# Score products of two heads' keys per partition half, and diagonal blocks of 192 columns, in a kernel of two attention layers and two linear-attention layers

## The chip, the core and the metric

The kernel runs on one core of a Trainium2 chip. The core has a matrix engine (TensorE, PE in the profile, with its weight loads listed apart as PEld), a vector engine (VectorE, DVE), a scalar engine that evaluates functions such as exp (ScalarE, ACT), a general engine (GpSimd, POOL), a queue engine that issues transfers (SyncE, SP), and 16 DMA engines. Products land in PSUM, which the kernel uses as four buffers of 128 partitions x 1024 four-byte values. The metric is the device time of one execution in microseconds (us).

## What is computed

The reference applies four layers to 2048 tokens of width 512: an attention layer A, a linear layer B, and both once more. Each layer is `x = x + layer(layernorm(x))`. A has 32 heads of 16 and works in four segments of 512 tokens. Cut to what matters here:

```
logits = einsum('bhqd,bhkd->bhqk', qs, ks) * scale + mask      # mask: -1e9 where key > query
p      = softmax(logits)
a_dot  = einsum('bhqk,bhkd->bhqd', p, vs)
a_mem  = (phi(qs) @ M) / (phi(qs) @ z + 1e-6)                  # M, z: sums over earlier segments
o      = g * a_mem + (1 - g) * a_dot                           # then o @ wo
M, z   = M + phi(ks)^T vs, z + sum(phi(ks))
```

The mask is causal inside a segment: of the 4 x 4 blocks of 128 queries by 128 keys, six lie wholly below the diagonal, four lie on it and need the triangle, and six are left out. B exponentiates projected keys and queries with both signs and contracts them over all tokens.

## The kernel before, in words

**How it is ordered.** The program is first written as a graph of operations (`Graph.op`), each with a planned duration, the tiles that it reads and writes, and the engines that may run it. `Graph.forward` then plays the graph with these durations and fixes the order on each engine and, where an operation may run on two engines, the engine. The list `STEPS` holds seeds: each moves some priorities before the last play (`Graph.moved`). `Graph.emit` writes the result out as one fixed instruction list per engine with semaphore waits. An operation marked `port` is not started by the planner on DVE while POOL works, and POOL is not given work while DVE runs such an operation. So a changed graph, planned duration or seed list gives a new order everywhere. The planner can also put in filler products (line 955) where PE would stand idle.

**Tiles.** Heads are taken in two sets `hp` of 16 heads; a set has two groups `gg` of 8 heads, 8 x 16 = 128 partitions. Partitions 0 to 63 hold four heads (half `b` = 0), 64 to 127 the other four. Nearly every product uses 64 partitions only, and two products, one per half, are issued together (a pair) and run at the same time in the two halves of the array.

**Scores, in `a_att` (line 1041).** For query block `i` (128 queries), group `gg` and key block `j <= i`, one pair of products writes the tile `S` in PSUM: 128 keys on the partitions, 2 halves x 4 heads x 128 queries = 1024 columns. The weights are 128 columns of `KT` (all four heads' keys of the half); the streamed side is `Q4`, in which each of the four heads has its own 512-column copy of the queries with the other three heads' partitions zero (lines 1000 to 1012: by a DMA into zeroed tiles for all segments but the first, by a DVE product with a mask `M4` for the first). ACT then writes `exp(0.25 S)` into a tile `PT` (line 1066, recorded at line 633). For `j == i`, POOL zeroes what lies above the diagonal with two `affine_select` operations of 128x512 (line 1070). There are 320 such tiles in the program, 2 layers x 4 segments x 4 groups x (1+2+3+4), and 128 of them are diagonal.

**Values.** Once all `PT` tiles of a set `hp` are there, the `PV` products (line 1092, 34 columns each, weights from `PT`, values `VT` streamed) run in two phases, in which the two partition halves of the keys swap places; the result is normalised by DVE (lines 1095 to 1099), transposed by a DMA (line 646), multiplied with `wo` and added to `X`.

**Buffers.** Of 27 tiles of 128x1024 in pool `p2`, at most 14 may be `PT`; `S` has at most 2 of the four PSUM buffers.

**Other work on the engines.** ACT also evacuates some projections, does the exps of B and copies (line 641, 633); POOL also does two small operations per layer norm (lines 886 and 888); SP issues all transposes and copies in one order.

## Time and profile before

| | |
|---|---|
| median of 4 runs | 534.22 us (530.71 to 537.62) |
| the profiled execution | 536.28 us, of which the profile's span is 534.4 us |
| granted TensorE clock, mean | 0.992 of full speed |
| instructions | 24584 |

The profile comes from one execution. "Busy" of PE counts a product from its start to its modelled end, and products overlap, so a busy PE may still have room. The chain of waits follows the work that ended last back to the start. A group of instructions carries the line that recorded it, and nearly all products are recorded at line 623, so groups are told apart by the tiles: `pQ,pK` are the scores, `pV,p` the value products.

### The profile page before, as it was taken

What the parts mean: (1) busy time and instruction counts of PE and PEld (TensorE: products, weight loads), DVE (VectorE), ACT (ScalarE), POOL (GpSimd) and SP (SyncE); (2) the same over time, 40 slices, a digit from 0 to 9 for tenths busy, and PEclk for the clock granted to TensorE, in tenths of its full rate; (3) what the DMA queues carried; (4) which work ended last, traced back from release to release, by engine and by line L of the source; (5) the groups of instructions that cost most, each with busy time, mean ns of one, the idle gap of its engine ahead of it and who ended that gap; (6) DMA issues with size and microseconds to landing.
All of it is one profiled execution on the core that took longest, in us unless ns stands there. A gap on an engine that the chain in (4) does not pass through costs nothing.

```text
span 534.4 us, 24584 instructions
## 1 busy us (share of the span) xinstructions
PE 474.2 (89%) x11148; PEld 279.5 (52%) x11148; DVE 437.9 (82%) x856; ACT 464.3 (87%) x543; POOL 231.7 (43%) x401
## 2 busy tenths in 40 slices
PE   6888977889989898999898997989989989999986
PEld 2435443454555464556656554555555546565674
DVE  5699994998977776786898998899888788887872
ACT  2699986799999999866988999999999999957993
POOL 5494994043753654200207734663564474320000
PEclk9999998999999999999999999999999999999999
DMA  4306743533111012000024434422311111100254
GB/s 125 114 13 137 163 124 86 91 43 82 42 43 42 15 36 39 12 2 2 5 61 98 93 78 74 63 57 57 72 33 29 49 22 23 33 12 3 53 120 130
DMA packets 89624, 31.77 MB, mean 59 GB/s; under 512 B 76688, under 2 KB 89520, under 8 KB 89520
## 3 DMA queue, kind: packets, MB, share of 16 engines
q1 hardware_dynamic: 89456, 30.17, 26.6%
q8 instruction: 88, 1.44, 1.2%
q14 instruction: 16, 0.13, 0.1%
q0 software_dynamic: 64, 0.02, 0.0%
HBM read 6.32 MB, written 2.10 MB: 16 GB/s over the span
## 4 chain that ended last, share of the span: by engine, by line
PE 44%; ACT 21%; DVE 19%; DMA 9%; SPq 3%; issue 2%; POOL 2%; ACTq 0%; POOLq 0%
PE D L623 42%; ACT p L633 18%; DMA p<-p 6%; DMA pX<-p 2%; DVE p L1098 2%; DVE stats L878 2%; SPq L646 1%; DVE pV L642 1%; DVE p L642 1%; DVE X L1131 1%; DVE p L899 1%; DVE pS L1176 1%; POOL p L1070 1%; DVE p L1271 1%; DVE pS L679 1%
## 5 line engine op out<-in xcount | busy, mean ns | idle before, releaser
L633 ACT ACTIVATE p<-D 128x1024 bf16<-128x1024 f32 (+1 forms) x420 | 401.1, 1030 | 38.9 <-PE D L623 35.4
L1070 POOL TENSOR_SCALAR_AFFINE_SELECT p<-p 128x512 bf16<-128x512 bf16 x256 | 162.4, 661 | 140.9 <-ACT p L633 140.2
L623 PE MATMUL D<-pQ,pK 64*128 64x512 bf16 x678 | 124.2, 378 | 8.7 <-ACT p L633 6.4
L623 PE MATMUL D<-pV,p 64*128 64x34 bf16 (+1 forms) x5316 | 93.6, 177 | 5.6 <-DVE X L1131 1.8
L623 PEld LDWEIGHTS D<-pV,p 64*128 64x128 bf16 x5316 | 81.9, 93 | 21.1 <-POOL p L1070 5.0
L886 POOL TENSOR_SCALAR rstd<-mv 128x1 f32<-128x1 f32 x60 | 17.9, 300 | 95.1 <-DVE mv L879 92.4
L623 PEld LDWEIGHTS D<-pQ,pK 64*128 64x128 bf16 x678 | 32.8, 93 | 40.6 <-ACT p L633 20.5
L1098 DVE TENSOR_TENSOR p<-D,pS 128x256 bf16<-128x256 f32 x112 | 46.7, 420 | 2.5
L623 PE MATMUL D<-WA_o,p 64*128 64x256 bf16 x512 | 39.4, 270 | 8.6 <-DMA p<-p 4.4
L1176 DVE TENSOR_REDUCE pS<-p 128x64 f32<-128x1024 bf16 (+1 forms) x36 | 38.8, 1090 | 8.4 <-ACT p L633 8.3
L878 DVE BATCH_NORM_STATS2 stats<-X 128x6 f32<-128x512 bf16 x64 | 43.3, 682 | 1.8 <-ACT X L641 1.1
L623 PE MATMUL D<-WB_o,p 64*128 64x256 bf16 x512 | 37.9, 270 | 5.4 <-DMA p<-p 4.3
L1196 DVE TENSOR_TENSOR pT<-D,pT 128x1024 bf16<-128x1024 f32 x32 | 38.7, 1216 | 3.6 <-PE D L623 3.3
L623 PE MATMUL D<-WB_k,pX 64*128 64x512 bf16 (+1 forms) x288 | 33.8, 353 | 5.7 <-DMA pX<-p 3.2
L888 POOL TENSOR_TENSOR rstd<-rstd,mhalf 128x1 f32<-128x1 f32 x60 | 34.5, 581 | 3.7
L623 PE MATMUL D<-WA_v,pX 64*128 64x512 bf16 x256 | 33.1, 377 | 2.7 <-DVE p L1098 1.0
L623 PE MATMUL D<-WB_v,pX 64*128 64x512 bf16 (+1 forms) x290 | 33.6, 353 | 1.1 <-DVE X L1131 0.4
L623 PEld LDWEIGHTS D<-WA_o,p 64*128 64x128 bf16 x512 | 21.7, 94 | 23.5 <-DMA p<-p 9.2
L623 PE MATMUL D<-pX,WB_q 64*128 64x512 bf16 x256 | 32.6, 377 | 0.3
L1131 DVE TENSOR_TENSOR X<-X,D 128x512 bf16<-128x512 bf16 x32 | 21.9, 683 | 13.2 <-PE D L623 13.0
L642 DVE CAST p<-D 128x1024 bf16<-128x1024 f32 (+2 forms) x27 | 26.2, 970 | 7.4 <-PE D L623 7.2
L679 DVE RECIPROCAL pS<-D 128x32 f32<-128x32 f32 (+1 forms) x64 | 20.7, 325 | 13.9 <-PE D L623 13.5
(115 smaller groups left out, 692.1 us busy)
## 6 DMA issues: line engine op xcount, KB each, us to landing
pQ<-p SPq DMA_DIRECT2D x56, 64.0 KB, 1.9
out_dram<-X SPq DMA_DIRECT2D x16, 128.0 KB, 2.0
X<-in_A_x_dram SPq DMA_DIRECT2D x3, 512.0 KB, 6.1
pX<-in_B_wqkv_dram SPq DMA_DIRECT2D x3, 512.0 KB, 4.5
p<-p SPq DMA_TRANSPOSE x76, 2.5
pX<-p SPq DMA_TRANSPOSE x54, 2.4
X<-in_A_x_dram SPq DMA_DIRECT2D x4, 128.0 KB, 2.9
pX<-in_A_wk_dram SPq DMA_DIRECT2D x2, 256.0 KB, 4.3
```

The costliest lines, as they stand in the source:

```text
L623: ins = e.matmul(out_ap, lhsT, rhs, start=st, stop=sp, tile_position=(basep(lhsT), 0))
L633: return self.g.op({"act": (dur, lambda e: e.activation(out_ap(), in_ap(), func, scale=scale))}, reads, writes, opens, label=label)
L642: "dve": ((340 if fast else n / 0.96 + 65), lambda e: e.tensor_copy(out_ap(), in_ap()))}
L679: return e.reciprocal(o, i)
L878: v(lambda e: e.bn_stats(self.stats[:, t, :], self.X[:, t, :]), 602, [R("X", t)], [R("st", t)], label="bn")
L886: v(lambda e: e.tensor_scalar(rs, self.mv[:, t, 1:2], LN_EPS, None, op0=ALU.add), 170, [R("mv", t)], [R("rstd", t)], eng="pool", label="rstd")
L888: v(lambda e: e.tensor_tensor(rs, rs, self.mhalf[:], ALU.pow), 540, [R("rstd", t), R("mhalf")], [R("rstd", t)], eng="pool", label="rstd")
L1070: v(lambda e, pt4=pt4: e.affine_select(pt4(), pt4(), [[0, 4], [1, 128]], ALU.is_ge, 0.0, base=0, channel_multiplier=-1), 560, [PT], [PT[hh ...
L1098: v(lambda e, pvv=pvv, rden=rden, part=part, dst=dst, k=k: e.tensor_tensor(part(dst), pvv()[:, :, k, :, 0:16], rden()[:, :, k, :, None].to ...
L1131: self.v(lambda e: e.tensor_tensor(xt(), xt(), res(), ALU.add), 602, [R("X", t), ps], [R("X", t)], label="res")
L1176: fn = lambda e, sgn=sgn, ev=ev, Z=Z, nz=nz: e.tensor_reduce(Z.t[:, sgn * nz:(sgn + 1) * nz], ev().rearrange("p (h d) -> p h d", d=16), AX ...
L1196: v(lambda e, Vt=Vt, src=src, vt=vt: e.tensor_tensor(vt(Vt, 0, 16), src(), vt(Vt, 16, 17).to_broadcast([128, 2, 2, 2, 16, 8]), ALU.mult), ...
```

## The change

Three things are redone around the scores, and buffers, planned durations and seeds go with them.

*Keys instead of queries are masked.* `KT` becomes a passing tile. The four heads of a half are split into two pairs. A new tile `KD` (128x2048) holds, for every 128 keys, twice 128 columns: the early 64 keys once for each head pair, then the late 64 keys once for each, with the other pair's partitions zero. Two `tensor_scalar` operations write it (POOL or DVE). The queries `Q2` (128 x 2 x 2 x 512) have two copies instead of four. One product then gives 64 keys for two pairs of heads at once, so a block below the diagonal takes two pairs of products of 256 columns instead of one of 512. In the result the partition half says both which 64 keys and which head pair a row is.

*Diagonal blocks are narrower.* The early 64 keys meet 128 queries, the late 64 keys only the later 64, so a half has 2 x 192 columns, `exp` covers 768 columns instead of 1024, and the columns that are never written stay zero in four tiles `PD` of their own, zeroed once. The triangle is added before the exp by a third pair of products: `II` (two stacked identities) times `far` (0 or -32768).

*Values for swapped halves.* Half of the heads now need their values in the other partition half. A DMA copies them from `VT` to a new tile `VU`, in pieces of 34 values (68 bytes).

```diff
+    def scores(self, S, PT, KD, Q2, gg, j, i):
+        c, n = gg * 1024 + j * 256, i * 128
+        def phases():
+            def item(b, m):
+                half = lambda x: x[64 * b:64 * b + 64]
+                q, k = half(Q2.t)[:, gg], half(KD.t)
+                if j < i:
+                    return S.t[:, 512 * b + 256 * m:512 * b + 256 * m + 256], k[:, c + 128 * m:c + 128 * m + 128], q[:, :, n:n + 128], m == 0, m == 1
+                out = S.t[:, 512 * b:512 * b + 384].rearrange("p (k c) -> p k c", k=2)
+                if m == 0:
+                    return out[:, :, 64:192], k[:, c:c + 128], q[:, :, n:n + 128], True, False
+                if m == 1:
+                    return out[:, :, 0:64], k[:, c + 128:c + 256], q[:, :, n + 64:n + 128], False, False
+                return out[:, :, 0:128], half(self.II), half(self.far)[:, None, :].to_broadcast([64, 2, 128]), False, True
+            return [[tuple(item(b, m) for b in range(2)) for m in range(2 if j < i else 3)]]
...
+            self.act(lambda: PT.t[:].rearrange("p (b k c) -> p b k c", b=2, k=2)[:, :, :, 64:256],
+                     lambda: S.t[:].rearrange("p (b c) -> p b c", b=2)[:, :, 0:384].rearrange("p b (k c) -> p b k c", k=2),
+                     ACT.Exp, 768, [S], [PT], scale=0.25, label="exp")
...
-                    PT = PTs[(gg, j)] = self.T(self.p2, "PT")
-                    self.mm(lambda S=S, KT=KT, Q4=Q4, j=j, gg=gg: [[tuple(
-                        (S.t[:, b * 512:(b + 1) * 512], KT.t[64 * b:64 * b + 64, gg * 512 + j * 128:gg * 512 + (j + 1) * 128],
-                         Q4.t[64 * b:64 * b + 64, gg, :, i * 128:(i + 1) * 128], True, True) for b in range(2))]],
-                        [[512]], [KT, Q4[("i", gg, i)] if (L, s) in MASKED else (Q4, ALLKEYS)], [S], opens=[PT], label="S")
-                    self.act(lambda PT=PT: PT.t[:], lambda S=S: S.t[:], ACT.Exp, 1024, [S], [PT], scale=0.25, label="exp")
-                    if j == i:
-                        for hh in range(2):
-                            pt4 = lambda PT=PT, hh=hh: PT.t[:, hh * 512:(hh + 1) * 512].rearrange("p (h q) -> p h q", h=4)
-                            v(lambda e, pt4=pt4: e.affine_select(pt4(), pt4(), [[0, 4], [1, 128]], ALU.is_ge, 0.0, base=0, channel_multiplier=-1),
-                              560, [PT], [PT[hh]], eng="pool", label="mask")
+                    PT = PTs[(gg, j)] = self.T(self.p2, "PT") if j < i else self.T(self.pP, "PD")
+                    self.scores(S, PT, st["KD"][hp], st["Q2"][hp], gg, j, i)
...
+            for m in range(2):
+                def fn(e, KT=KT, KD=KD, m=m, raw=raw):
+                    dst = KD.t[:].rearrange("p (t x c) -> p t x c", x=4, c=64)
+                    dst = dst[:, :, 0::3] if m else dst[:, :, 1:3]
+                    return e.tensor_scalar(dst, KT.t[:].rearrange("p (t x c) -> p t x c", x=2, c=64), self.MK[:, 0 if raw else 1, m:m + 1], None, op0=ALU.mult)
+                self.g.op({"pool": (1250.0, fn), "dve": (600.0, fn)}, [KT, R("MK0") if raw else R("MK1")], [KD[m]], label="KD", port=True)
...
-                for b in range(2):
-                    for i in range(4):
-                        fn = lambda e, Q4=Q4, QT=QT, i=i, b=b: e.tensor_tensor(
...
-                for a in range(0, 4, 2):
-                    fn = lambda e, Q4=Q4, QT=QT, a=a: [e.dma_start(Q4.t[sl::4, :, sl, :], QT.t[sl::4, :].rearrange("p (b q) -> p b q", b=2)) for sl in (a, a + 1)]
+                    fn = lambda e, Q2=Q2, QT=QT, k=k: e.tensor_scalar(Q2.t[:, :, k, :], QT.t[:].rearrange("p (b q) -> p b q", b=2), self.MQ[:, k:k + 1], None, op0=ALU.mult)
...
+                fn = lambda e, Q2=Q2, QT=QT: [e.dma_start(Q2.t[k::2, :, k, :], QT.t[k::2, :].rearrange("p (b q) -> p b q", b=2)) for k in range(2)]
...
+            self.dma(lambda tp=tp: [(VU.t[64 - 64 * h:128 - 64 * h, 2 * tp:2 * tp + 2].rearrange("p t (u r) c -> p t u (r c)", r=2),
+                                     VT.t[64 * h:64 * h + 64, 2 * tp:2 * tp + 2].rearrange("p t (u k r) c -> p t u k (r c)", k=2, r=2)[:, :, :, 0])
+                                    for h in range(2)], 2, [VT[2 * tp], VT[2 * tp + 1]], [VU[2 * tp], VU[2 * tp + 1]], label="Vx", lat=4000.0)
...
-N_XT, N_Q4, N_K1, N_K2, N_VT, N_SM, N_KT = 5, 3, 12, 27, 5, 6, 4
+N_XT, N_Q4, N_K1, N_K2, N_VT, N_SM, N_KT, N_PD = 5, 3, 12, 23, 5, 6, 4, 4
-CAP2 = {"PT": 14, "EQ": 16, "ET": 8, "phe": 2, "phiKT": 2, "QT": 2, "PhK": 2, "phiQ": 4}
+CAP2 = {"PT": 7, "EQ": 16, "ET": 8, "phe": 2, "phiKT": 2, "QT": 2, "KT": 2, "PhK": 2, "phiQ": 4}
```

Not printed: the setup of `II`, `far`, `MQ`, `MK` and of the zeros in `PD`; the index arithmetic of `PV`, which reads the new places; planned durations of loads (520 to 560, 620 to 640) and of the two POOL operations of a layer norm (170 to 240, 540 to 560); and `STEPS`, whose 148 seeds are replaced by 212 others. The instruction lists of the two kernels count:

| engine | before | after | what differs most |
|---|---|---|---|
| PE | 11150 | 12006 | scores 678 to 1312, triangle 256, fillers and warm-up 170 to 132 |
| ACT | 545 | 550 | 128 of the 320 attention exps are 128 x 4 x 192; more copies of weights, fewer of `X` |
| DVE | 858 | 848 | 16 masked query products go, 4 `KD` and 4 `Q2` come |
| POOL | 405 | 186 | 256 selects go, 28 `KD` come |
| SP | 239 | 243 | query copies 56 to 28, value copies 32 |

## The prediction, made before the changed kernel had run

> **What bounds the kernel now.** The first view is the page's busy times, with the chain that ended last.
>
> ```profile
> PE 474.2 (89%) x11148; PEld 279.5 (52%) x11148; DVE 437.9 (82%) x856; ACT 464.3 (87%) x543; POOL 231.7 (43%) x401
> PE 44%; ACT 21%; DVE 19%; DMA 9%; SPq 3%; issue 2%; POOL 2%; ACTq 0%; POOLq 0%
> L1070 POOL TENSOR_SCALAR_AFFINE_SELECT p<-p 128x512 bf16<-128x512 bf16 x256 | 162.4, 661 | 140.9 <-ACT p L633 140.2
> ```
>
> Three engines are above 80%, so the average names no bound. The second view, busy time by stage, does (columns: stretch, its length, busy us and calls of each engine, clock, DMA share, GB/s).
>
> ```profile
> 27.00:75.00 48.00, 42.24 (x990) 22.70 (x988) 45.67 (x99) 47.04 (x54) 39.57 (x66) 1.00 0.48 104
> 75.00:95.00 20.00, 13.16 (x184) 5.85 (x178) 11.87 (x21) 13.96 (x15) 10.90 (x18) 0.91 0.47 108
> 107.00:160.00 53.00, 48.33 (x1238) 28.19 (x1232) 47.48 (x88) 51.63 (x56) 27.28 (x46) 1.00 0.28 52
> 160.00:214.00 54.00, 47.44 (x1276) 28.03 (x1272) 39.87 (x75) 51.16 (x55) 27.05 (x48) 1.00 0.16 33
> 267.00:320.00 53.00, 49.06 (x1055) 30.07 (x1049) 48.81 (x107) 47.80 (x59) 24.50 (x46) 1.00 0.37 82
> 320.00:374.00 54.00, 48.23 (x1138) 27.44 (x1136) 48.64 (x98) 51.28 (x55) 29.37 (x50) 1.00 0.35 64
> 374.00:427.00 53.00, 48.64 (x1270) 28.84 (x1266) 44.95 (x79) 51.49 (x55) 27.70 (x48) 1.00 0.23 46
> 427.00:455.00 28.00, 25.41 (x744) 15.35 (x744) 22.82 (x44) 27.84 (x31) 17.00 (x31) 1.00 0.14 22
> 455.00:481.00 26.00, 25.47 (x584) 15.35 (x582) 22.49 (x38) 20.12 (x23) 6.75 (x13) 1.00 0.10 23
> ```
>
> The numbers are PE, PEld, DVE, ACT, POOL. In the six stretches 107-214 and 267-455, 295 us together, ACT works 281.2 us, 95%: it is the bound there, with 13.8 us idle. In 27-75 ACT (98%) and DVE (95%) are. In 75-95 no engine is: in the chain of waits SP's queue (75.0 to 81.0) and a transpose (3.64 us from 81.08) stand there. In 455-481 PE is. How full PE really is needs the third view, products back to back in the timeline (start, duration).
>
> ```profile
> 377.60 0.96 PE L623 MATMUL D<-pV,p 64*128 64x34 bf16 x64
> 380.76 1.04 PE L623 MATMUL D<-pX,WA_q 64*128 64x512 bf16 x8
> 393.57 0.61 PE L623 MATMUL D<-WA_o,p 64*128 64x256 bf16 x8
> ```
>
> Eight products are four pairs: 0.43 us more for 4 x 256 more columns is 0.42 ns a column, and 0.61 us less 4 x 107 ns leaves 0.18 us, one tail, with nothing per pair. Thirty-two pairs of 34 columns take 0.96 us, 25 ns a pair after the tail. Counting every form of each stretch by these two rules, max(0.42 ns x columns, 25 ns) a pair, PE needs 44.7, 43.4, 46.2, 44.7, 45.4 and 22.2 us in the six ACT-bound stretches: 246.6 of 295, 84% (1.4 of it fillers), and 24.2 of 26, 93%, in 455-481, the fullest stretch seen.
>
> **The change part by part**, against the profiled execution: 536.28 us, span 534.4, so 1.9 lies around the span, and it is 2.06 above the median of the runs.
>
> *Narrower exps.* The ACT rows for one operation on PSUM:
>
> ```profile
> L633 ACT ACTIVATE p<-D 128x1024 bf16<-128x1024 f32 x412 | 396.6, 1038 | 35.3 <-PE D L623 31.9
> L633 ACT ACTIVATE p<-D 128x512 bf16<-128x512 f32 x8 | 4.8, 598 | 3.7 <-PE D L623 3.5
> ```
>
> 440 ns for 512 columns, so 768 cost 818 ns, 220 less, and 128 of them 28.2 us of ACT. The selects of line 1070, two to a diagonal tile, say where: 36, 38, 25, 34, 38 and 25 in the six stretches, 98 tiles, **-21.6 us**; 32 in 27-75, 16 tiles, **-3.5**; 14 tiles where ACT has room, 0. The row with four pieces of 192 columns is not in the trace; copies in pieces of 64 columns (597 ns for 512, 21 whole `X` evacuations also 597) show no price for pieces.
>
> *Work moved to ACT.* By shape: 8 more weight copies (657 ns), 3 more normalisations (830), 3 more `pX` (597) and others +3, against 7 fewer `X` (597), 3 fewer 1024-column evacuations and 3 of 512: about +4 us, half of it before 27 us where ACT has room: **+2** (0 to 4).
>
> *Scores on PE.* A diagonal tile streams 256+128+256 columns instead of 512: 128 x 0.42 = 53 ns, and 98 tiles in the ACT-bound stretches are 5.2 us. A block below the diagonal has the same columns in two pairs instead of one, 0 by the rows above. Without fillers PE then needs 246.6 - 1.4 + 5.2 = 250.4 us in the 273.4 left, 92%, about the fullest seen, so I charge most of it: **+5** (0 if ACT's slack hides it; 15 in the rival below). The tiling page of the Trainium skill (TensorEngine Tiling (Array Packing), Instruction Overhead) speaks against the change: it gives each product some 60 cycles of overhead. For 128 x 2 + 192 = 448 more pairs of 60 x 0.42 ns that is an estimated 11 us, and the sum would stand up to that much higher. The 0.61 us row above leaves no room for it at 256 columns, and I go by the row.
>
> *The selects.* They free 162.4 us of POOL. What waited on them (us, times, longest; the third row is POOL waiting):
>
> ```profile
> PEld D L623 <- POOL p L1070: 7.9, 16, 1.4
> ...
> PE D L623 <- POOL p L1070: 1.9, 4, 0.9
> POOL rstd L886 <- DVE mv L879: 92.4, 25, 26.2
> ```
>
> PE lost at most 9.8 us, and POOL has 2% of the chain, 10.7 us, partly because the layer norm's two POOL operations queue behind selects. Behind the select the exp itself is next late for the value products, and an ACT-bound stretch gives nothing for POOL: **-3** (0 to -10.7). In the timeline a DVE `tensor_scalar` of 128x1024 took 0.80 us at 383.27 with a select running and 0.42 us at 399.37 with POOL idle, but DVE is behind ACT in every stretch, so that relief counts 0 (to -4: 48 such rows at about 80 ns over 0.42). The Trainium skill (SBUF — State Buffer, SBUF: two separate sides) says that POOL and a two-port DVE operation lock each other out for the whole instruction. By that rule `KD` would still block DVE; the sum is the same while ACT binds.
>
> *`KD`.* 28 on POOL, 4 on DVE. One POOL operation of 1024 elements: 1.3 us by the select (661 ns for 512), 3.1 by the WA_v product (1526 for 512, two inputs); one input, so 1.3: 36 us on an engine left with 69. A layer norm's POOL pair can queue behind two of them, 2.6 us, as behind a tile's two selects now. Scores now wait for it behind the `KT` evacuation; keys are projected a segment ahead, so cover is tens of us, except at the start, where DVE's 128x1024 row (501 ns) twice is uncovered: **+1** (0 to 3). DVE loses 16 x 525 ns of masked queries for 4 x 0.5 of `Q2` and 4 x 0.5 of `KD`, 4.4 us, in 27-75 where it is second to ACT: 0 (to -3).
>
> *Transfers.* SP issues 32 value copies for 28 fewer query copies (0.63 us each by the timeline), +2.5 us over the program, each queue entry waiting for a `V` evacuation with transposes behind it. Each has 64 x 2 x 8 = 1024 pieces.
>
> ```profile
> q1 hardware_dynamic: 89456, 30.17, 26.6%
> p<-p SPq DMA_TRANSPOSE x76, 2.5
> ```
>
> 26.6% of 16 x 534.4 us for 89456 packets is 25 ns each, so a copy occupies the engines 1.6 us and should land near 2.5 us like a transpose (1.9 to 6.1, the fastest and slowest median in that list), and all 32 raise the DMA share from 27% to some 36%. It hurts where DMA is full, 45-65 (0.85 to 0.95 busy in stretches of 10 us): four copies, 6.5 us of DMA time: **+2** (0 to 6.5).
>
> *Buffers.* 14 `PT` become 7 plus 4 `PD`. For the last query block a set `hp` holds 6 + 2, leaving 1 + 2, 1.04 + 2 x 0.82 = 2.7 us of exps, to cover two value phases of 0.96 us with a gap, 2.1 us; before, 6 free tiles covered 6.2 us against two selects and the phases, 3.4 us. 16 such places (2 layers x 4 segments x 2 sets); I charge 0.12 us each: **+2** (0 to 22).
>
> Sum: -21.6 - 3.5 + 2 + 5 - 3 + 1 + 2 + 2 = -16.1: 520.2 for such an execution, **518** for the median. The new order everywhere has no row; its luck is in the range.
>
> **The rivals.**
> *PE takes over.* If PE cannot pass 87% (46.2 of 53 in 267-320, where ACT has 5 us idle), 250.4 us need 288, and the six stretches give 7 us instead of 21.6 - 5; with the other terms (-3.5, +2, -3, +1, +2, +2) the sum is -6.5: 528. For: 44% of the chain is PE. Against: 93% was reached.
> *All of it passes.* PE hidden, no charge for buffers or transfers, the whole POOL share gone: -21.6 - 3.5 + 2 + 1 - 10.7 = -32.8, 501; with half of POOL's 507; I take 504. For: PE has 16% free. Against: the idle PE time that selects ended is only 9.8 us.
> *Starved exps (slower).* If the value products start late, ACT runs out of `PT` tiles at the 16 places. Place: between the last exp of one set and the first free tile. It decides above the 0.6 us of cover left; to cancel 16.1 us and end 1% slower (+5.4) it needs 21.5/16 = 1.3 us a place beyond that, so value products 1.9 us late: 540; 547 if 2.4 us late. For: PE sits 92% full and serves in a fixed order. Against: ACT has 464 - 320 x 1.038 = 132 us of other operations to put there.
> *The narrow exp is not narrow.* If four pieces cost as much as 1024 columns, 25.1 us go and +9 stays: 543. The 64-column copies speak against it.
>
> **How the numbers follow.** Forecast 518 (own range 509 to 527): 0.50. PE takes over, 528 (523 to 534): 0.18. All passes, 504: 0.14. Starved, 540 to 547 (a quarter of it within 1%): 0.12. Not narrow, 543: 0.06. One per cent, about what a measurement tells from no change, is 528.9 to 539.6. Faster: 0.48 (0.02 kept for an unlucky new order) + 0.09 + 0.14 = 0.71. Same: 0.02 + 0.09 + 0.03 of the starved case = 0.14. Slower: 0.09 + 0.06 = 0.15. The range runs from 502, inside `All passes`, to 540, where the slower cases begin; some 0.04 lies below and 0.14 above.
>
> **What would show it.** Right: a row 128x768 near 818 ns; ACT busy near 440; PE's stretches fuller than 90%; POOL near 105 us; value copies landing near 2.5 us. Wrong: exps waiting on PE far above 35.4 us in total (PE or buffers), `KD` or value copies among the releasers of score or value products, DMA share above 0.4, or an exp row near 1 us.

## The result, and the profile after

The changed kernel takes 537.73 us (median of 44 runs, 532.71 to 543.77) against 534.98 us for the kernel before on the same chips (63 runs, 529.31 to 541.10). The ratio is 1.0061 with a 95% interval of 1.0043 to 1.0079: some 3.3 us slower, where the prediction had 16 us faster; 537.7 lies inside its range of 502 to 540, but at the slow end, near the rivals that end slower and not near the forecast of 518. Ratios leave out executions more than 1.5% above the fastest of the same kernel, medians keep them. The profiled execution took 541.04 us, 3.3 above the median, and has a span of 539.0 us. Its busy times and its chain of waits, from the page:

```profile
PE 476.8 (88%) x12004; PEld 320.6 (59%) x12004; DVE 433.4 (80%) x846; ACT 442.9 (82%) x548; POOL 152.4 (28%) x182
...
PE 48%; DVE 20%; ACT 13%; DMA 7%; POOL 6%; issue 5%; SPq 0%; POOLq 0%
```

ACT fell by 21 us, to 442.9, as forecast (near 440), and its share of the chain from 21% to 13%. Yet the span grew. The time that ACT gave up shows as idle time in the stretches where it had been 95% busy (same columns as in the prediction: PE, PEld, DVE, ACT, POOL, then clock, DMA share, GB/s):

```profile
27.00:75.00 48.00, 38.71 (x925) 26.61 (x927) 39.07 (x85) 35.83 (x43) 28.04 (x36) 0.89 0.76 133
320.00:374.00 54.00, 48.88 (x1271) 33.66 (x1272) 46.49 (x92) 46.42 (x54) 18.40 (x21) 1.00 0.40 60
374.00:427.00 53.00, 47.86 (x1262) 32.60 (x1256) 42.55 (x80) 43.43 (x49) 13.31 (x13) 0.97 0.27 48
```

ACT is idle for 9.6 us of 53 in 374-427, where it had 1.5 to spare before, and PE is no fuller than before (47.86 against 48.64). In 27-75 every engine has room, PE too; the TensorE clock there is 0.89 in the place of 1.00 and the DMA share 0.76 in the place of 0.48. So no engine's load explains the span, and the next view is what the engines wait for (total us, times, longest):

```profile
ACT p L634 <- PE D L624: 48.8, 51, 4.1
PEld D L624 <- issue: 39.2, 56, 2.5
POOL pK L1005 <- DVE p L643: 24.9, 8, 11.3
...
ACT pP L634 <- PE D L624: 20.0, 25, 4.7
PE D L624 <- issue: 17.5, 17, 1.8
```

Exps wait for PE for 68.8 us in the place of 35.4. And PE itself waits 17.5 us for "issue", which means that nothing in the profile, no semaphore above all, held it; before this row read 4.6 us, 7 times, and that of its weight loads (PEld) 28.3 us, 45 times. Among the groups of instructions two rows answer to terms of the forecast:

```profile
L634 ACT ACTIVATE pP<-D 128x768 bf16<-128x768 f32 x128 | 101.3, 823 | 21.3 <-PE D L624 20.0
...
L1005 POOL TENSOR_SCALAR pK<-p,MK 128x1024 bf16<-128x1024 bf16 x28 | 81.8, 2931 | 35.5 <-DVE p L643 24.9
```

The narrow exp is as narrow as forecast (823 ns, forecast 818). A `KD` operation on POOL takes 2.93 us, not 1.3; the planner has it at 1.25. In the chain of waits (start, us) it stands at the start and again later, and so do the gaps without a semaphore (six of its longest are shown; all together they are 5.4% of the chain, 2.4% before):

```profile
18.48 11.91 POOL pK L1005 x4
...
45.79 1.75 issue
...
276.35 5.67 POOL pK L1005 x2
...
329.85 1.41 issue
...
384.56 1.82 issue
...
430.65 1.27 issue
...
444.24 1.21 issue
...
473.10 1.44 issue
```

What such a gap is, the timeline of PE shows (start, us, operation, idle time before it):

```profile
384.31 0.20 PE L624 MATMUL D<-pU,pP 64*128 64x34 bf16 x4
384.36 0.20 PE L624 MATMUL D<-pV,pP 64*128 64x34 bf16 x3
386.38 0.21 PE L624 MATMUL D<-pV,pP 64*128 64x34 bf16 x1 [1.82 <-issue]
386.38 0.27 PE L624 MATMUL D<-pU,pP 64*128 64x34 bf16 x4
```

PE stops in the middle of a row of value products, between two that wait for nothing, for 1.8 us. The transfers of the instruction queue say why:

```profile
q8 instruction: 94, 1.54, 1.3%
```

94 transfers of 16 KB for 24008 weight loads and products of PE: a transfer brings 256 instructions (before: 88 for 22296). Counting PE's instructions in the trace in order (weight loads, products, waits), twelve of the 25 gaps above 0.7 us in which PE runs none of these, the six shown among them, end at exactly the same place of a block of 256 (position 193 of the count modulo 256), where chance would put one in 256; and in all twelve the first instruction comes 1.33 to 1.50 us after a transfer of 16 KB has ended. There a new block begins, and PE has run out of instructions. In the kernel before, none of 13 such gaps lies at this position. Added up over all block starts with a gap above 0.1 us that is 18 gaps and 17.5 us, against 7 and 2.4 us before. By the busy times PE is idle for 62.2 us of 539.0, and was for 60.2 of 534.4. Outside of block starts its idle time therefore fell, from some 58 to some 45 us: in these two executions the waits elsewhere shrank by about as much as the block starts added.

Some of the gaps are followed by a lower clock. Around the gap that ends at 386.38 the trace shows (stretch, its length, busy us and calls of PE, PEld, DVE, ACT, POOL, then clock, DMA share, GB/s):

```profile
382.90:386.30 3.40, 1.66 (x130) 1.55 (x121) 1.69 (x2) 1.12 (x2) 2.80 (x2) 1.00 0.22 68
386.30:389.70 3.40, 3.32 (x36) 1.73 (x38) 2.20 (x7) 0.59 (x1) 3.26 (x2) 0.51 0.02 5
```

The clock is granted at half speed for 3.4 us. That happens six times inside this span (from 27.9, 34.8, 48.4, 106.4, 386.3 and 475.1 us) and, its last 1.3 us aside, twice in the kernel before (from 10.8 and 85.9); three of the six begin within 1 us of the end of one of the twelve gaps (47.54, 386.38 and 474.53). The mean clock is 0.981 in this execution, 0.992 in the one before; over all executions on record with their clock it is 0.987 (44) and 0.993 (114 of the kernel before). That difference alone is an estimated 3.4 us of 537, as much as the two kernels differ by. No run separates what a gap costs by itself from what the clock after it costs.

### The profile page after: what moved, and what is told of

Same layout as the page of the kernel before. It is cut to its first block, busy times and chain, and to the rows that moved or that the text cites. A ratio compares the mean times of both kernels' runs of the same rounds, so it can differ in the third digit from the quotient of the medians.

```text
span 539.0 us, 26034 instructions
## 1 busy us (share of the span) xinstructions
PE 476.8 (88%) x12004; PEld 320.6 (59%) x12004; DVE 433.4 (80%) x846; ACT 442.9 (82%) x548; POOL 152.4 (28%) x182
## 3 DMA queue, kind: packets, MB, share of 16 engines
q1 hardware_dynamic: 122288, 32.40, 34.7%
## 4 chain that ended last, share of the span: by engine, by line
PE 48%; DVE 20%; ACT 13%; DMA 7%; POOL 6%; issue 5%; SPq 0%; POOLq 0%
PE D L624 48%; ACT p L634 9%; DMA p<-p 4%; POOL pK L1005 3%; ACT pP L634 2%; DVE p L1150 2%; DMA pX<-p 2%; DVE p L1323 2%; DVE p L643 2%; DVE stats L896 2%; DVE pT L1248 1%; DVE p L917 1%; DVE p L953 1%; DVE pS L680 1%; DVE p L955 1%
## 5 line engine op out<-in xcount | busy, mean ns | idle before, releaser
L634 ACT ACTIVATE p<-D 128x1024 bf16<-128x1024 f32 (+1 forms) x292 | 282.4, 1019 | 50.9 <-PE D L624 48.8
L624 PE MATMUL D<-pQ,pK 64*128 64x256 bf16 (+1 forms) x1312 | 118.5, 264 | 15.9 <-ACT p L634 4.2
L634 ACT ACTIVATE pP<-D 128x768 bf16<-128x768 f32 x128 | 101.3, 823 | 21.3 <-PE D L624 20.0
L1005 POOL TENSOR_SCALAR pK<-p,MK 128x1024 bf16<-128x1024 bf16 x28 | 81.8, 2931 | 35.5 <-DVE p L643 24.9
L624 PE MATMUL D<-pU,p 64*128 64x34 bf16 x1536 | 59.6, 176 | 2.4 <-issue 1.6
L624 PE MATMUL D<-pV,pP 64*128 64x34 bf16 x1024 | 50.2, 176 | 4.0 <-issue 4.0
L624 PEld LDWEIGHTS D<-pV,p 64*128 64x128 bf16 x1728 | 50.1, 93 | 6.0 <-issue 4.9
L624 PE MATMUL D<-pU,pP 64*128 64x34 bf16 x1024 | 50.0, 176 | 0.6 <-DVE nb L911 0.3
L624 PEld LDWEIGHTS D<-pU,p 64*128 64x128 bf16 x1536 | 45.7, 93 | 6.5 <-issue 2.3
L624 PE MATMUL D<-far,II 64*128 64x256 bf16 x256 | 36.7, 277 | 0.7 <-DVE stats L896 0.7
```

The source lines that it names most:

```text
L624: ins = e.matmul(out_ap, lhsT, rhs, start=st, stop=sp, tile_position=(basep(lhsT), 0))
L634: return self.g.op({"act": (dur, lambda e: e.activation(out_ap(), in_ap(), func, scale=scale))}, reads, writes, opens, label=label)
L1005: return e.tensor_scalar(dst, KT.t[:].rearrange("p (t x c) -> p t x c", x=2, c=64), self.MK[:, 0 if raw else 1, m:m + 1], None, op0=ALU.mult)
```

## The experiments

The theories at the start: (a) ACT was the bound, and the gain was eaten by something new: the slow `KD`, the instructions of PE, the value copies; (b) ACT was never the bound, and the narrow exp is worth little. Except for the one run planned anew, all kernels keep the planned durations and so the order on every engine of the kernel that they start from. Ratios are to the kernel before, run on the same chip; "us" differences are differences of ratios times 535.

**1. The narrow exp alone, in the kernel before.**

```diff
-  self.act(lambda PT=PT: PT.t[:], lambda S=S: S.t[:], ACT.Exp, 1024, ...)
+  nw = 768 if j == i and (L == 1 or s >= 2) else 1024
+  self.act(lambda PT=PT, nw=nw: PT.t[:, 0:nw], lambda S=S, nw=nw: S.t[:, 0:nw], ACT.Exp, 1024, ...)
```

> The kernel before in its own order, with one edit: the exp of a diagonal tile takes 768 of its 1024 columns in 96 of the 128 tiles (those of layer 1's last two segments and of layer 2). The last 256 columns of those tiles are left as the buffer has them, so that part of the attention is not computed. Nothing else moves: this is the worth of the narrower exp alone. The forecast (ACT is the bound where these tiles lie, 215 ns each) expects -15 to -20 us against the kernel before. The rival that PE, near full, takes over at once expects no more than -7 us. That the narrow exp costs what the wide one does is already excluded by the 823 ns row of the changed kernel.

Measured 535.86 us, ratio 0.9965 (0.9926 to 1.0004): -1.9 us, an interval that just includes no change.

```profile
PE 471.5 (88%) x11148; PEld 278.6 (52%) x11148; DVE 437.3 (82%) x856; ACT 448.2 (84%) x543; POOL 232.5 (44%) x401
```

```profile
ACT p L633 <- PE D L623: 52.2, 77, 3.5
```

(busy times, then the waits.) ACT's busy time fell by 16.1 us, and its wait for PE rose from 35.4 to 52.2: the time came back as waiting, almost whole. Theory (b) holds for the kernel before in its own order; an order made for the narrow exp alone was not tried.

**2. More products for the same columns, in the kernel before.**

```diff
-  (S.t[:, b * 512:(b + 1) * 512], ..., Q4.t[64 * b:64 * b + 64, gg, :, i * 128:(i + 1) * 128], True, True)
+  (S.t[:, b * 512 + 256 * m:b * 512 + 256 * m + 256], ..., Q4.t[64 * b:64 * b + 64, gg, 2 * m:2 * m + 2, i * 128:(i + 1) * 128], m == 0, m == 1)
```

> The kernel before in its own order, with every 512-column score product issued as two of 256: the same columns streamed, the same result, 678 products more (and their weight loads). The forecast's row (nothing per product beyond its columns) expects 0 to +2 us. The theory that PE's instruction supply or a price per product (60 cycles each would be 25 ns, 8 us for 339 pairs) makes up for a good part of the lost gain expects +6 to +15 us, with more PE idle time under 'issue'.

Measured 545.63 us, ratio 1.0151 (1.0101 to 1.0201): +8.1 us. The score group, and PE's gaps among the waits:

```profile
L623 PE MATMUL D<-pQ,pK 64*128 64x256 bf16 x1356 | 126.0, 274 | 10.9 <-ACT p L633 8.5 <-ACT WB_k L641 0.8 <-issue 0.5
```

```profile
PE D L623 <- issue: 11.7, 9, 2.5
```

The products themselves cost 1.8 us more (126.0 against 124.2), 5 ns a pair: the forecast's row holds. The rest is not in the products' rows, and "issue" rose from 4.6 to 11.7.

**3. `KD` as copies; 4. `KD` on DVE, planned anew.** 
```diff
+  if e is self.nc.gpsimd:                                   # run 3
+      return e.tensor_copy(dst, src)
   return e.tensor_scalar(dst, src, self.MK[:, 0 if raw else 1, m:m + 1], None, op0=ALU.mult)
...
-  self.g.op({"pool": (1250.0, fn), "dve": (600.0, fn)}, ..., label="KD", port=True)
+  self.g.op({"dve": (480.0, fn)}, ..., label="KD", port=True)      # run 4
```

> The changed kernel in its own order, with the 28 key products on POOL made plain copies of the keys (the mask is left out there, so a score takes both heads' keys; the four on VectorE stay). If a copy with one input and no scalar is near the 1.3 us I had taken, POOL falls by some 45 us and what the long KD cost by itself shows: the theory that the late KD lost the gain expects -8 to -14 us against the changed kernel, most of it in the first 60 us and at the three later places where the chain of waits has KD (11.9 + 5.7 + 3.3 + about 5 us). The rivals (PE's instruction supply, value copies, the order) expect -3 to 0. If the copy takes as long as the product, this run says nothing.

> The changed kernel planned anew with KD on VectorE alone at 0.48 us (28 more there, +13.5 us of VectorE, which stands at 433 us, and -82 us of POOL). The theory that the slow KD on POOL is the main loss expects 8 to 14 us less than the changed kernel, so 524 to 530. The rivals expect 534 to 545, a new order included, since VectorE then has 447 us of work.

The copies: 534.6 us, ratio 0.9969 (0.9943 to 0.9996), 4.9 us below the changed kernel. The row shows that they took 1.1 us, a little less than the 1.3 that I had taken for the product:

```profile
L1007 POOL COPY pK<-p 128x1024 bf16<-128x1024 bf16 x28 | 30.4, 1110 | 43.1 <-DVE p L643 28.0 <-ACT p L642 15.0
```

The newly planned kernel took 596.15 us, ratio 1.1119 (1.1077 to 1.1161). It says nothing of `KD`: run 12 below makes the same move in the old order and gains. With another duration the seeds of `STEPS` move other priorities, and the order that they had been picked for is gone. That loss is larger than every effect in this study, and it is why the later runs leave the order alone.

**5. No selects in the kernel before; 6. with the narrow exp.** 
```diff
-  e.affine_select(pt4(), pt4(), [[0, 4], [1, 128]], ALU.is_ge, ...)
+  e.affine_select(pt4()[:, 0:1, 0:8], pt4()[:, 0:1, 0:8], [[0, 1], [1, 8]], ALU.is_ge, ...)
```

> The kernel before in its own order, with its 256 selects cut to 8 elements each (the causal triangle is left out). The worth of removing the selects alone. The forecast charged -3 us, bounds 0 to -10.7. A theory that the selects' latency sits on PE's path, so that the gain of the narrow exp can't show without them, expects -5 us or more here and more in the next run than both alone; the theory that PE's own stream is the bound expects -4 to 0.

> Both edits together in the kernel before: 96 of the 128 diagonal exps narrow, the selects cut to 8 elements (triangle left out, 256 columns of the 96 tiles as the buffer has them). If the two hide each other (the exp's end no longer ends a select's wait), this gains more than the sum of the two runs alone, -10 us or more. If PE's stream and its fixed order are the bound, -2 to -6 us, about the sum.

533.07 us, 0.9956 (0.9926 to 0.9987), -2.4 us; and both together 531.82 us, 0.9928 (0.9897 to 0.9958), -3.9 us: the sum of the two (-4.3). They don't hide each other. The selects' term (-3) lies inside the interval of run 5.

**7. One product for a tile below the diagonal, in the changed kernel; 8. value copies in large pieces.**

```diff
+  if m is None:
+      return S.t[:, 512 * b:512 * b + 512], k[:, c:c + 128], q[:, None, :, n:n + 128].to_broadcast([64, 2, 2, 128]), True, True
...
-  VT.t[64 * h:64 * h + 64, 2 * tp:2 * tp + 2].rearrange("p t (u k r) c -> p t u k (r c)", k=2, r=2)[:, :, :, 0]
+  VT.t[64 * h:64 * h + 64, 2 * tp:2 * tp + 2, 0:H // 2]
```

> The changed kernel in its own order, with each score tile below the diagonal as one product of 512 columns again (with one half's keys for all four heads, so the other half's keys are left out): the same columns, 192 pairs fewer. If the price per product that the split of the kernel before showed (8 to 9 us for 339 pairs) is PE's supply of instructions, 4 to 6 us less than the changed kernel and fewer 'issue' gaps on PE (17.5 and 39.2 us now). If that price was an accident of the split's timing, -1 to +1 us.

> The changed kernel in its own order, the 64 value copies with the same bytes, but 128 pieces of 544 B in the place of 1024 of 68 B (the heads land in wrong places, so the value products of half the heads use others' values). The queue's waits and order stay; only the load on the transfer engines goes. The theory that the small pieces slow the transposes and the instruction fetches expects -4 to -8 us and a DMA share near 27%; the forecast's charge was 2 us; the other theories expect 0.

One product: 530.48 us, 0.9903 (0.9867 to 0.9940), 8.5 us below the changed kernel, with "issue" on PE down from 17.5 to 7.0:

```profile
PE D L625 <- issue: 7.0, 10, 1.5
```

Flat copies: 538.95 us, 1.0055 (1.0025 to 1.0086), no difference, though the copies landed in 2.1 us in the place of 3.1. The small pieces cost nothing; what the 32 copies cost by their places in SP's queue, which this run keeps, was not tried.

**9. A triangle of 8 columns; 10. no triangle product; 11. about half of the saved exp time given back; 12. `KD` moved to DVE in the same order.**

```diff
-  return out[:, :, 0:128], half(self.II), half(self.far)[:, None, :].to_broadcast([64, 2, 128]), False, True
+  return out[:, :, 0:8], half(self.II), half(self.far)[:, None, 0:8].to_broadcast([64, 2, 8]), False, True    # run 9; run 10: range(2) products
...
+  e.activation(S.t[:, 384:448], S.t[:, 0:64], ACT.Exp, scale=0.25)                                            # run 11, ahead of each diagonal exp
...
+  for o in order:                                                                                            # run 12, when the order stands
+      if o.label == "KD" and o.eng == "pool":
+          o.eng = "dve"
```

> The changed kernel in its own order, the triangle's product over 2 x 8 columns in the place of 2 x 128 (the rest of the causal triangle is left out): the number of products stays, the columns fall by 128 x 240. If PE pays for columns, as the rows of the kernel before say (0.42 ns each, less a floor of 25 ns a pair: 82 ns for each of 128), 5 to 10 us less than the changed kernel. If what costs is the number of instructions, 0 to -3 us here, and the rest in the next run.

> The changed kernel in its own order without the triangle's product (the causal triangle is left out): 128 pairs, 256 products and 512 PE instructions fewer as well as the columns. The price per instruction that the one-product run showed (7 us for 192 pairs, 37 ns each) expects some 5 us less than the run with 8 columns, and the 'issue' gaps on PE (17.5 and 39.2 us) lower; a price by columns alone expects 0 to -3 us beyond that run (25 ns a pair).

> The changed kernel in its own order, each of the 128 diagonal exps followed on ScalarE by one more of 64 columns, near 0.21 us by the 512 and 1024 rows, which gives back the time that the narrow exp saved (27 us of ScalarE); the result is the same. If the narrow exp is worth what I forecast once the order is made for it, 12 to 21 us more than the changed kernel. If PE is the bound there too, 1 to 6 us more.

> The changed kernel with the 28 key products of POOL issued by VectorE at the place where the order had them on POOL; nothing else moves (no new plan, unlike the run with KD on VectorE alone, whose new plan lost 58 us). At 0.48 us each in the place of 2.93. By the copies' run (1.1 us each: -5 us) 5 to 8 us less than the changed kernel, so 530 to 533, a little below the kernel before. If VectorE waits at these places for ScalarE's evacuations and holds up its queue, 0 or a loss.

| run | median, us | ratio to before | against the changed kernel |
|---|---|---|---|
| 9, 8 columns | 535.98 | 1.0057 (1.0024 to 1.0090) | -0.2 us |
| 10, no triangle product | 530.65 | 0.9930 (0.9893 to 0.9967) | -7.0 us |
| 11, half the exp time given back | 538.95 | 1.0109 (1.0079 to 1.0139) | +2.6 us |
| 12, `KD` on DVE | 532.57 | 0.9971 (0.9941 to 1.0002) | -4.8 us |

Runs 9 and 10 belong together. Taking 94% of the triangle's columns away gives nothing; taking its 512 PE instructions away as well gives 7 us (some 3 of these could be the 128 pairs' own 25 ns):

```profile
L624 PE MATMUL D<-far,II 64*128 64x16 bf16 x256 | 23.0, 170 | 0.4 <-DVE p L1150 0.4
```

```profile
PE D L624 <- issue: 14.8, 14, 2.4
```

```profile
PE D L624 <- issue: 5.4, 7, 1.4
```

(the triangle's group in run 9, then PE's gaps in run 9 and in run 10). Run 11 gave ACT back 12.7 us of busy time, about half of the 27 that I had reckoned: in the trace the 128 small operations, 236 ns each, overlap the exps beside them. It cost 2.6 us. In run 12 DVE did the 32 `KD` in 465 ns each, 13 us more, and yet its busy total stayed at 433.3, since other rows of its own got shorter, most of all the 48 `tensor_scalar` of 128x1024, from 23.3 to 19.4 us; that this is because POOL had less to do is my reading. One of the two groups of 24 (changed kernel, then run 12):

```profile
L954 DVE TENSOR_SCALAR p<-p 128x1024 bf16<-128x1024 bf16 x24 | 11.8, 496 | 0.0
```

```profile
L957 DVE TENSOR_SCALAR p<-p 128x1024 bf16<-128x1024 bf16 x24 | 9.7, 408 | 0.0
```

**13. 30% of the value products out, in the kernel before; 14. with the narrow exp; 15. waits in the triangle's place.** Run 14 is run 13 with the edit of run 1, run 15 is run 10 with this.

```diff
-  r = [[(item(p, 0, gg, hl, j, p), ...) for gg in range(2) for j in range(i + 1) for hl in range(4)]
+  r = [[(item(p, 0, gg, hl, j, p), ...) for gg in range(2) for j in range(min(i, 1), i + 1) for hl in range(4)]
...
+  for _ in range(o.more):              # run 15: 8 satisfied waits, two to an instruction, ahead of a diagonal score tile
+      eng.wait_ge(*past)
```

> The kernel before in its own order, its value products left out for the first key block of every query block but the first (1536 of 5120 products, 30%; that part of the attention is missing; the exps and scores stay). PE's work falls by 768 pairs, 19 us at 25 ns. If ScalarE is the bound of the kernel before, as I forecast from its 95% in the six stretches, 0 to -5 us. If PE (its stream and its supply of instructions, 3072 of them) is the bound, -15 to -25 us.

> The same with the narrow exps of the first run (96 of the 128 diagonal tiles over 768 columns; the rest as the buffer has it). If PE's relief has made ScalarE the bound, the narrow exp, worth 1.9 us alone, is now worth 8 to 20 us against the run with fewer value products. If neither engine's load but the fixed order with its waits sets the time, 2 us again.

> The changed kernel without the triangle's product (the causal triangle is left out), with 512 more instructions on PE in its place: four waits on semaphores that have long been reached, ahead of each diagonal score tile (each an instruction without work in the array). If the number of instructions on PE is what costs, whatever they do, the gain of 7 us of the run without the triangle is gone: 536 to 540. If the price is one of products in the array (a weight load and a pass through it), 530 to 532. A wait may cost PE's sequencer time of its own, so a result above 540 doesn't tell fetch from sequencer.

Run 13: 525.25 us, 0.9764 (0.9708 to 0.9819), -12.6 us. Run 14: 521.54 us, 0.9698 (0.9652 to 0.9743), 3.5 us more, with intervals that overlap. Run 13 took an estimated 19 us of stream from PE and gained 12.6 while ACT stayed 88% busy; the narrow exp took 16.1 us from ACT in run 1 and 15.6 in run 14 and gained 1.9 and 3.5. So in this order PE's work counts for far more than ACT's. Both answers lie between the two that I had put down; that each engine waits for the other in turn in a fixed order would explain it, but no run shows that by itself. Run 15: 547.21 us, 1.0171 (1.0119 to 1.0224), above the 540 from which, as said beforehand, it can't tell the supply of instructions from the time that PE's sequencer takes for a wait.

**16. All three losses out at once; 17. with about half of the exp time given back.** The edits of runs 7, 10 and 12 in one kernel, then that of run 11 on top.

> The changed kernel in its own order with the three found losses taken out at once: KD of POOL issued by VectorE at the same places, each score tile below the diagonal as one product (one half's keys left out), no triangle's product (the causal triangle left out). Alone they gave 4.8, 7 and 7 us. If they are separate losses, 517 to 521, which is what I forecast for the change; if they are one and the same slack, 528 to 531.

> The same with the exp of 64 more columns on ScalarE for each of the 128 diagonal tiles (near 0.2 us each, 17 to 27 us of ScalarE), the same work left out. If the narrow exp has the forecast's worth once PE is relieved, 10 us or more above the run without it. If it is not worth more than in the changed kernel (2.6 us), 1 to 5 us: then the forecast's main term is wrong in this order whatever PE does.

530.03 us, 0.9896 (0.9865 to 0.9927): 8.8 us below the changed kernel, not the 20 of the three alone (4.8, 7.0, and 8.5 for run 7, where the expectation says 7). And 530.91 us (523.05 to 535.93), 0.9816 (0.9764 to 0.9867), with the exp time given back as in run 11: no loss. So a price per product, 37 ns as run 10's expectation has it, was wrong as a theory too: with 1280 instructions fewer than in the changed kernel, gaps of PE were back that runs 7 and 10 had lost.

```profile
q8 instruction: 89, 1.46, 1.3%
```

```profile
PE D L628 <- issue: 12.2, 12, 2.0
```

That led to the count of positions told above, and to the last run. The gaps at block starts, counted in each trace (one execution of each kernel; the times are those of all):

| kernel | PE instructions at block starts: gaps, us | time against before, us |
|---|---|---|
| before | 7, 2.4 | 0 |
| 1, narrow exp | 6, 3.4 | -1.9 |
| 2, scores split | 9, 8.4 | +8.1 |
| changed | 18, 17.5 | +3.3 |
| 3, `KD` as copies | 18, 17.0 | -1.7 |
| 8, flat value copies | 17, 15.7 | +2.9 |
| 9, triangle of 8 columns | 16, 13.2 | +3.0 |
| 11, half the exp time given back | 15, 12.6 | +5.8 |
| 7, one product below the diagonal | 10, 6.6 | -5.2 |
| 10, no triangle product | 8, 5.4 | -3.7 |
| 12, `KD` on DVE | 17, 14.4 | -1.6 |
| 16, all three out | 13, 9.5 | -5.6 |

The changed kernel and runs 3, 8, 9 and 11 have the same number of PE instructions and so the same borders; their gaps still run from 12.6 to 17.5 us, and their times don't follow them. So the count is no price list, and a difference of some 5 us in it can come without a border moved.

The theory for the last run: whether a block of 256 runs dry depends on where its border falls. Value products are issued at 25 ns a pair, so a block that held only these would be used up in some 1.6 us (64 pairs), while one with more long products lasts until the next block is there. It is not the whole cause: in the kernel before, two blocks in which 115 and 118 of the 128 products are value products were used up in 3.07 and 3.10 us without a gap. There the next transfer had started 0.47 us after the block's start and 0.03 us before it, in the changed kernel's twelve long gaps 0.65 us after it or later. What makes it start late is not shown.

**18. The borders shifted, all else as in run 12.** The 56 warm-up products at the start are split in two, the same columns: 112 more instructions ahead of everything else.

```diff
-  for _ in range(2):
+  for n in range(4):
       for b in range(2):
-          ins = e.matmul(ps.t[:, 512 * b:512 * b + 512], ones(b), ...to_broadcast([64, 4, 128]), ...)
+          c = 512 * b + 256 * (n % 2)
+          ins = e.matmul(ps.t[:, c:c + 256], ones(b), ...to_broadcast([64, 2, 128]), ...)
```

> The kernel with KD issued by VectorE (532.6), its 56 warm-up products of 512 columns at the start issued as 112 of 256: the same array time, the same result, and 112 more instructions on PE ahead of everything else. Counted in the trace, PE's queue (weight loads, products, waits) has its long gaps without a semaphore at the starts of blocks of 256 instructions (the 193rd of every block, 17 gaps of 14.4 us together there, 18 of 17.5 in the changed kernel, 7 of 2.4 in the kernel before), each 1.3 to 1.5 us after a 16 KB instruction transfer ended. The 112 shift all later blocks by almost half. If the place of these borders in the dense value products costs the time, the gaps lie elsewhere and, by the intervals of the trace with at least 3.5 us from one block's start to the next, come to some 10 us in the place of 15: 526 to 529, 1.2 to 1.7% below the kernel before. If the number of instructions costs wherever the borders lie, 532 to 534.

528.74 us, ratio 0.9872 (0.9832 to 0.9913), in the forecast's 526 to 529: 5.3 us below run 12 by nothing but 112 more instructions, at nearly the same mean clock over the executions (0.989, in run 12 0.990). The gaps at block starts are 9 of 6.7 us in the place of 17 of 14.4, a larger drop than the spread just told. The gain comes late in the program: the first update of `X` by a layer starts at 57.2 us, 3.3 later than in run 12, the last one of 32 at 471.4, 6.7 earlier.

```profile
PE D L627 <- issue: 8.9, 8, 2.6
```

```profile
381.88 0.20 PE L627 MATMUL D<-pU,pP 64*128 64x34 bf16 x4
381.93 0.20 PE L627 MATMUL D<-pV,pP 64*128 64x34 bf16 x4
381.98 1.02 PE L627 MATMUL D<-WB_v,pX 64*128 64x512 bf16 x8
```

These are the same value products as in the timeline of the changed kernel at 384 to 386.6 us, where a gap of 1.82 us stood among the last of them (1.55 us in run 12); here they run through to the next projection. This version leaves nothing out, and it is 1.3% faster than the kernel before and 1.9% faster than the changed one.

## Why the prediction was wrong, step by step

**The step that failed first is "it is the bound there", said of ACT in the six stretches, and the -21.6 us that I took from it in full.** ACT was 95% busy there, and the exp did become 215 ns shorter. But the kernel before with the narrow exp alone got 1.9 us for 16.1 us less work of ACT, where run 13 got 12.6 for 19 less of PE's; and giving about half of the time back cost 2.6 us in the changed kernel and nothing in run 17. Here a busy share near 1 did not mean that the other engines would run ahead once ACT was faster: PE was 84% full by the stream, and in run 1 the time that ACT gave up came back as ACT's wait for PE. I had the number that spoke against it, the chain's 44% on PE against 21% on ACT, and set it aside for the busy shares.

**The second is the price of products: "0 by the rows above" and +5 for the columns.** It was wrong both ways. The columns cost nothing that shows (run 9), and the products' own time is as the row said (run 2, 5 ns a pair). What the sum has no term for is PE's supply of instructions: at block starts PE has 15 us more of gaps than before. That such gaps cost time is shown by run 18, which moves the borders and little else: 5.3 us for 7.7 us of gaps, 0.7 us for each. Runs 7 and 10, which also take work out, got 8.5 for 10.9 and 7.0 for 12.1, but run 9 got 0.2 for 4.3. By the rate of run 18 the 15 us are an estimated 10 of the 19 that I missed; how many they are in fact stays open. So does why there are more of them: the changed kernel has 896 score products more, another order, and transfers that start later in their blocks, and no run tells these apart. The page of the Trainium skill that I had weighed, TensorEngine Tiling (Array Packing), section "Instruction Overhead", gives 60 cycles per product. Run 2 looks like it, 8.1 us for 339 pairs, 24 ns a pair; but the products' rows grew by 5 ns a pair only, and the gaps at block starts by 6.0 us. That run was not tried with its borders shifted.

**The third is `KD` "one input, so 1.3".** It measured 2.93 us. I had 3.1 as the other end, from a row with two operands, and chose the select because it was nearer in kind; the mask is a second operand, if one value per partition, and the row with two operands was the nearer one. Moving `KD` away gives 4.8 us (run 12; run 3 with copies at 1.1 us: 4.9) where I had charged 1. Most of the chain's part is at the start, where the four `KD` take the 11.9 us at 18.48 and the layer norms' POOL operations stand behind them; in run 12 the first update of `X` starts at 53.9 us in the place of 59.4. That the planner had counted 1.25 us may be why it put them there.

**Right:** the exp's row, ACT's total, the selects (-3; run 5 -2.4), the direction of the DMA share (26.6% to 34.7%, I had 36%). **Signs that failed:** POOL near 105 us (152.4, by the slow `KD`), value copies landing near 2.5 us (3.1), PE's stretches fuller than 90% (below). **Charged for nothing:** the small pieces of the value copies (+2; run 8 shows 0). **Not settled:** the buffers' +2 was never tried alone. And the terms don't add up: with an estimated 10 us for the gaps and the 4.8 of `KD` taken away, the changed kernel would stand 11 to 12 us below the kernel before, while the selects and the exp alone give 3.9 in the old order. The losses need not add (run 16), the clock is in none of the terms, and the new order has a part that no run separates, because every new plan is a new order (run 4).

Of the rivals, *PE takes over* was the nearest in its sign, "exps waiting on PE far above 35.4 us" (68.8). Its condition, that PE cannot pass 87%, is not what happened: counted by the prediction's two rules, PE's products need 82 to 85% of the changed kernel's five long stretches between 107 and 427 us (without 214 to 267), where the forecast had 92%, and 90% in two of the same stretches of run 18. So PE was held off by its gaps and waits before its stream was full. Its price left out the supply of instructions, which the profile before hardly shows: 4.6 us of "issue", and 2.4 us at block starts. *Starved exps* was not tested: no run changes the number of `PT` tiles.

## What to carry to other kernels

Before a busy engine is called the bound, take some of its work away in the unchanged order: one run here would have shown 2 us where the busy share promised 20. Where PE issues rows of very short products, look at idle time that no semaphore ends, count the instructions, and see whether it falls on borders of 256: then a few more instructions at the start can be worth more than a change of the algorithm. And a change to a kernel with a searched order is measured together with its new order; to learn what a part is worth, change it with the order held fixed.

## What the runs showed of the hardware

PE's instructions came in transfers of 16 KB, 256 at a time. In the twelve long gaps of the changed kernel the transfer of the next block started 0.65 to 3.8 us after the start of the block before, in eight of them within 1.2 us, it lasted 0.9 to 1.7 us, and the first instruction followed 1.33 to 1.50 us after its end. So in this program PE ran dry while all data were there. Three of these gaps ended within 1 us of the start of 3.4 us at half the clock.

A multiplication with one value per partition took POOL 2.93 us for 128x1024 two-byte elements, a plain copy of the same shape 1.11 us, and DVE did the multiplication in 0.47 us. Pieces of 68 bytes in the 32 value copies (the expectation of run 8 counts 64, two to an operation) slowed nothing that the time shows, with 122288 packets on the queue in the place of 93616 in run 8.

The planner keeps `port` operations of DVE and POOL apart, and the page SBUF — State Buffer of the Trainium skill, section "SBUF: two separate sides", has the loser of the two blocked for the whole instruction. The timeline of the changed kernel's start shows them at work together (POOL's four `KD`, then DVE's four masked queries):

```profile
18.48 11.92 POOL L1005 TENSOR_SCALAR pK<-p,MK 128x1024 bf16<-128x1024 bf16 x4
```

```profile
26.04 3.30 DVE L1028 TENSOR_SCALAR pQ<-p,MQ 128x1024 bf16<-128x1024 bf16 x4
```

The four masked queries one by one (shortest, median and longest in ns):

```profile
L1028 DVE TENSOR_SCALAR pQ<-p,MQ x4: 474/868/1328, 26.0 to 28.9; 128x1024 bf16<-128x1024 bf16 x4
```

DVE began at 26.04 and was done before POOL was. Two of its four operations took 474 and 477 ns, as long as in run 12 without POOL beside them (467 to 471), and two, around the border between two of POOL's at 27.4 us, took 1258 and 1328. Each is shorter than one of POOL's operations (2.84 us or more). So here DVE was slowed for a part of the time and not shut out for a whole POOL operation, as far as the spans of POOL in a trace can be trusted.
